# One exponential over two PSUM banks in place of two: a step of a state-space convolution kernel

## The chip, the cores and the metric

The program runs on one core of one Trainium2 chip. A core has a matrix engine (PE, with its weight loads shown apart as PEld), a vector engine (DVE), a scalar engine for activation functions (ACT), a general engine (POOL) and a queue that issues transfers (SP), each with its own instruction stream; they wait for each other by semaphores. Matrix products land in PSUM, which has eight banks of 512 float32 columns per partition. The metric is the device time of one execution in microseconds, lower is better.

## The reference

The reference is a block with adaptive layer norms around a diagonal state-space convolution (S4D) and a token-mixing MLP, in float32. This change touches the generation of the convolution kernel K, in `_A_ref`:

```python
def _A_ref(u, log_A_real, A_imag, C_real, C_imag, log_dt, D_skip):
    L = u.shape[1]                                   # L, D, N = 2048, 448, 256
    dt = jnp.exp(log_dt)
    A = -jnp.exp(log_A_real) + 1j * A_imag
    C = (C_real + 1j * C_imag) * dt[:, None]
    pos = jnp.arange(L)
    P = jnp.exp((A * dt[:, None])[:, :, None] * pos[None, None, :])
    K = 2.0 * jnp.einsum("dn,dnl->dl", C, P).real
    y = irfft(rfft(u_t, 2 * L) * rfft(K, 2 * L))[:, :, :L]
    return y + u * D_skip

h = layernorm(x) * (1 + ca) + sa
x = x + ga * _A_ref(h, ...)
h = layernorm(x) * (1 + cb) + sb
x = x + gb * mixer_mlp(h)        # W2 gelu(W1 LN(h)^T), over the tokens
```

## The kernel before, in words

The time axis is split as 32 x 64 positions, so that the exponential of a channel and state at any position is a product of a factor E (64 positions, complex) and a factor G (32 positions, complex), and K is a sum over states of E times G, a matrix product. The generator works through 56 **steps** s (28 groups of 16 channels, two halves of 128 states each). What one step does, with its lines:

- `st_exponents` (matmuls in `halves`, L627): PE computes from a short list of parameters (`lex`) and a table (`tab`) the exponents of the magnitudes, 512 columns for E (`xe`) and 512 for G (`xg`), each in a PSUM bank of its own.
- `st_exp` (L650): ACT takes the exponential of each, into `mag`, 128 x 2 x 512 in SBUF.
- `st_phase` (L627): PE computes the phases the same way into tiles of the same names, with eight matmuls of 512 columns that alternate between xe and xg; two pairs of them round the phase with a large constant (`mg`).
- `st_mag2` (L666, L671): POOL makes the magnitudes of the upper 32 positions of E, `m2`.
- `st_step`: ACT forms sines and cosines (L683 and L684 absolute values of xe and xg; L685 sine of xe, in place; L686 sine of xg into `gs`; L687 cosine for G in `gs`; L688 cosine for E, written over xg); POOL multiplies G (L690, L691); DVE multiplies E (L692, L693 with the sine, L695, L696 with the cosine). Between L693 and L695 `between()` lets DVE do work of other parts: evictions `yt` (L555) and `uo` (L589), products `z` (L817), and pieces of the parameter chains.
- `st_kgen` (L717): PE forms 64 small products of E and G in the bank `kg`; every second step ACT copies the bank out (L731).

Steps come in batches of 8. A **window** ahead of each batch computes all 8 magnitudes, since exponentials and sines need different function tables on ACT: it alternates `st_exponents` of the next step on PE with `st_exp` on ACT. In the batch, step s issues on PE the phase of step s + 1 and the kernel matmuls of step s - 2 (s - 1 after step 32), then ACT, POOL and DVE work of step s. Around this, other work is woven in by the order of the program: the transforms of the input u (L552, L585), the transforms of K (L755, copies L761), and from step 33 on the products in the frequency domain (`piece`: kx L809, z L817, vv L832, copies vt L842). The order on PE, ACT, DVE and POOL is that of the program text (`manual_schedule`); only SP's is chosen by the scheduler. After the generator (about 346 us) come the second half of the pieces and then the MLP.

PSUM is full: three banks for the transforms (`pms`), four for the tiles of the exponents and phases (`pph`, two names with two buffers each), one for kg. A tile's buffer is given to the next tile of that name when all that read or write the tile are done.

Of the kernel before, what the change touches and what calls it, by code (L numbers as in the profile page):

```python
# [11 lines left out]
F32 = mybir.dt.float32  # L12
F32R = mybir.dt.float32r
BF16 = mybir.dt.bfloat16
AF = mybir.ActivationFunctionType
# [7 lines left out]
P = 128  # L23
# [209 lines left out]
def tile_adaln_s4d_mixer(ctx, tc, i, out):  # L233
    nc = tc.nc
    x = i["A_u"][0]
# [17 lines left out]
    with ExitStack() as es:  # L253
        V, S, G, T = nc.vector, nc.scalar, nc.gpsimd, nc.tensor
# [13 lines left out]
        pph = kgen.enter_context(tc.tile_pool(name="pph", bufs=2, space=PSUM))  # L268
# [27 lines left out]
        tab = cg.tile([P, 3, 512], F32R, name="tab")  # L296
# [27 lines left out]
        lex = [cg.tile([P, N], F32R, name=f"lex{k}") for k in range(4)]  # L324
# [195 lines left out]
        nm = xp.tile([P, 16], F32, name="nm")  # L520
# [81 lines left out]
        mags, m2s, eg, phs = {}, {}, {}, {}  # L602
# [20 lines left out]
        def halves(out, lhs, rhs, start, stop):  # L623

            for k in range(2):
                r = slice(64 * k, 64 * k + 64)
                T.matmul(out[k], lhs[r], rhs[r], start=start, stop=stop)  # L627
# [12 lines left out]

        def st_exponents(s):
            g, h = divmod(s, 2)
            phs[s] = [pph.tile([P, 512], F32, tag=nm, name=nm) for nm in ("xe", "xg")]
            halves(phs[s], lex[g % 4][:, h * P : (h + 1) * P], tab[:, 2], True, True)

        def st_exp(s):
            mags[s] = mp.tile([P, 2, 512], F32, tag="mag", name="mag")
            pm = phs.pop(s)
            for k in range(2):
                S.activation(mags[s][:, k], pm[k], AF.Exp)  # L650

        def st_phase(s):

            g, h = divmod(s, 2)
            lhs = lph[g % 3][:, h * P : (h + 1) * P]
            pm = [pph.tile([P, 512], F32, tag=nm, name=nm) for nm in ("xe", "xg")]
            halves(pm, lhs, tab[:, 1], True, False)
            halves(pm, mg[:, 0], ones, False, False)
            halves(pm, mg[:, 1], ones, False, False)
            halves(pm, lhs, tab[:, 0], False, True)  # L660
            phs[s] = pm
# [347 lines left out]
        def window(s):  # L1009
# [9 lines left out]
            if s == 0:  # L1019
                st_exponents(s)  # L1020
            for e in range(BATCH):
                st_exp(s + e)

                if e + 1 < BATCH:
                    st_exponents(s + e + 1)
                else:
                    st_phase(s)
# [53 lines left out]
        for s in range(tail):  # L1081
# [30 lines left out]
            if s >= NHALF:  # L1112
                flush(dve)
                mellow()
            else:
                if s < 32 and s % BATCH > 1:
                    st_kgen(s - 2)
                if s % BATCH < 2:
                    warm(10)
                if (s + 1) % BATCH:  # L1120
                    st_phase(s + 1)
                elif s + 1 < NHALF:
                    st_exponents(s + 1)
                if s == 7:
                    warm(10)

                if s > 32 and s % BATCH:
                    st_kgen(s - 1)
                st_step(s, between)
# [122 lines left out]
    with ExitStack() as es:  # L1252
        es.enter_context(tc.manual_schedule(engines={ENG.PE, ENG.Activation, ENG.DVE, ENG.Pool}))
        V, S, G = nc.vector, nc.scalar, nc.gpsimd
# [212 lines left out]
```

## Time and profile before

| | |
|---|---|
| median of 3 runs | 696.14 us (693.27 to 698.49) |
| span of the profiled execution | 693.5 us; no other time of that execution is given |
| generator, seven batches of 8 steps | about 15 to 346 us of the span |
| exponentials L650 | 112 operations of 128x512, mean 614 ns (xe) and 617 ns (xg) |
| sines and absolute values L683 to L688 | 56 each, means of 604 to 645 ns |
| products of E on DVE, L692 to L696 | 56 each, means of 677 to 684 ns |
| PE, ACT, DVE, POOL busy | 91%, 64%, 63%, 39% of the span |

Busy times of an engine add up its operations even where they overlap; ACT operations that follow each other closely start 0.48 us apart and last 0.6. A row of the order of time gives the start (us from the span's start), the duration, the engine, the line, the operation and what it writes and reads; in square brackets stands idle time of the engine ahead of it, and what ended it. The chain of waits is the work that ended last, followed back from the end.

### The profile page before, as it was taken

To read this page: it belongs to the slowest core of one execution; us is meant where nothing else is said; L and a number is where in the kernel's file an instruction comes from. 1 tells how busy PE (TensorE), PEld (TensorE's weight loads), DVE (VectorE), ACT (ScalarE), POOL (GpSimd) and SP (SyncE) were. 2 spreads that over 40 slices of the span, in tenths; PEclk is the share of its full clock that TensorE was granted. 3 is DMA by queue.
4 is the path that set the end of the run, shared out by engine and by line. 5 is a ranking of instruction groups with operands and counts; after the bars stand their busy time and mean duration, and the time that the engine had idled before them with its cause. 6 is when DMAs were issued, how large, how long until landed. Compare 5 with 4: busy or idle time off the path is not lost.

```text
span 693.5 us, 19319 instructions
## 1 busy us (share of the span) xinstructions
PE 628.4 (91%) x7706; PEld 452.3 (65%) x7706; DVE 438.7 (63%) x835; ACT 446.6 (64%) x847; POOL 269.7 (39%) x349
## 2 busy tenths in 40 slices
PE   0878999999888889988898899999999999999997
PEld 0444555444345545555554567778899999999997
DVE  7886789789785574856745578876732364444441
ACT  5888598999689889989856768887322352222220
POOL 7694669588499667767635300000000000000000
PEclk9989999999999899999899999999999999999999
DMA  7595557598786354443479899955574445556540
GB/s 174 176 208 130 196 186 247 200 225 258 219 253 189 94 131 140 131 125 104 116 251 341 280 269 261 262 151 142 177 226 108 146 132 160 160 162 170 163 131 26
DMA packets 100322, 125.16 MB, mean 180 GB/s; under 512 B 13860, under 2 KB 81992, under 8 KB 100232
## 3 DMA queue, kind: packets, MB, share of 16 engines
q1 hardware_dynamic: 99288, 121.30, 61.0%
q0 software_dynamic: 944, 2.62, 1.6%
q8 instruction: 61, 1.00, 0.6%
q14 instruction: 29, 0.24, 0.1%
HBM read 88.53 MB, written 34.87 MB: 178 GB/s over the span
## 4 chain that ended last, share of the span: by engine, by line
PE 62%; ACT 12%; POOL 8%; DMA 6%; DVE 5%; issue 5%; SPq 1%; DVEq 0%; POOLq 0%; ACTq 0%
PE o L1434 7%; PE acc L1270 6%; PE o L1433 6%; PE o L1435 6%; PE acc L1271 6%; PE acc L1272 6%; PE xe L627 5%; PE kg L717 4%; POOL G L691 3%; POOL G L690 2%; PE xg L627 2%; PE vv L832 2%; PE kx L809 2%; PE kg L639 2%; PE y L1307 2%
## 5 line engine op out<-in xcount | busy, mean ns | idle before, releaser
L218 ACT CAST whi<-w 128x896 fp32r<-128x896 f32 x64 | 59.7, 938 | 134.3 <-PE o L1434 82.6
L227 DVE TENSOR_TENSOR wlo<-w,whi 128x896 fp32r<-128x896 f32 x64 | 68.1, 1085 | 40.6 <-ACT whi L218 40.6
L690 POOL TENSOR_TENSOR G<-mag,gs 128x512 f32<-128x512 f32 x56 | 71.8, 1282 | 46.0 <-ACT gs L686 45.9
L1270 PE MATMUL acc<-h3h,whi 128*128 128x448 f32 x224 | 82.9, 370 | 1.7 <-ACT h3h L1337 0.9
L1271 PE MATMUL acc<-h3l,whi 128*128 128x448 f32 x224 | 81.6, 364 | 0.2 <-DVE mean L1291 0.2
L1434 PE MATMUL o<-ul,whi 128*128 128x448 f32 x224 | 81.3, 363 | 0.0
L1433 PE MATMUL o<-uh,whi 128*128 128x448 f32 x224 | 81.2, 362 | 0.0
L1272 PE MATMUL acc<-h3h,wlo 128*128 128x448 f32 x224 | 80.7, 360 | 0.0
L1435 PE MATMUL o<-uh,wlo 128*128 128x448 f32 x224 | 80.6, 360 | 0.0
L717 PEld LDWEIGHTS kg<-E,G 128*32 128x32 f32 x3584 | 58.1, 117 | 31.7 <-issue 22.1
L717 PE MATMUL kg<-E,G 128*32 128x64 f32 x3584 | 68.2, 231 | 4.1 <-issue 4.1
L691 POOL TENSOR_TENSOR G<-mag,gs 128x512 f32<-128x512 f32 x56 | 71.8, 1281 | 0.0
L627 PE MATMUL xg<-tab,lph 64*128 64x512 f32 x112 | 62.9, 561 | 8.0 <-DVE E L696 3.5
L627 PE MATMUL xe<-tab,lph 64*128 64x512 f32 x112 | 63.6, 568 | 1.9 <-ACT gs L687 0.9
L1438 DVE TENSOR_TENSOR y<-o,x 128x448 f32<-128x448 f32 x16 | 10.0, 624 | 78.8 <-PE o L1435 78.8
L692 DVE TENSOR_TENSOR E<-m,xe 128x512 f32<-128x512 f32 x53 | 36.3, 684 | 35.2 <-ACT xe L685 25.1
L671 POOL TENSOR_TENSOR m<-mag,w 128x512 f32<-128x512 f32 x53 | 55.8, 1052 | 4.1
L1270 PEld LDWEIGHTS acc<-h3h,whi 128*128 128x128 f32 x224 | 42.0, 188 | 15.2 <-ACT h L1342 3.5
L817 DVE TENSOR_TENSOR z<-kx,u 128x448 f32<-128x448 f32 x48 | 28.4, 619 | 33.1 <-PE kx L809 30.5
L832 PE MATMUL vv<-z,si 64*64 64x224 f32 x512 | 36.8, 385 | 9.4 <-ACT yk L761 6.2
L627 PE MATMUL xe<-tab,lex 64*128 64x512 f32 x56 | 31.0, 569 | 15.7 <-POOL wm L874 14.8
L1433 PEld LDWEIGHTS o<-uh,whi 128*128 128x128 f32 x224 | 42.1, 188 | 3.4
(242 smaller groups left out, 1455.9 us busy)
## 6 DMA issues: line engine op xcount, KB each, us to landing
w<-in_B_w_dram SPq DMA_DIRECT2D x64, 224.0 KB
w<-in_B_w_dram SPq DMA_DIRECT2D x32, 448.0 KB
yu_d<-yt SPq DMA_DIRECT2D x16, 448.0 KB
yi<-yu_d SPq DMA_DIRECT2D x32, 224.0 KB
us_d<-uo SPq DMA_DIRECT2D x16, 448.0 KB
u<-us_d SPq DMA_DIRECT2D x64, 112.0 KB
v_d<-vt SPq DMA_DIRECT2D x32, 224.0 KB
vt<-v_d SPq DMA_DIRECT2D x14, 448.0 KB
```

The source lines that it names most:

```text
L218: self.nc.scalar.copy(hi, w)
L227: eng.tensor_tensor(lo, w, hi.bitcast(F32), ALU.subtract)
L627: T.matmul(out[k], lhs[r], rhs[r], start=start, stop=stop)
L690: G.tensor_tensor(Gt[:, 1], mg_, v32(sg), ALU.mult)
L691: G.tensor_tensor(Gt[:, 0], mg_, v32(cg_), ALU.mult)
L717: T.matmul(kg[32 * q : 32 * q + 32, m], Gt[:, c, d], E[:, c, d], start=h == 0 and c == 0 and m == 0, stop=h == 1 and c == 1, skip_group_ch ...
L1270: nc.tensor.matmul(acc[f], hi[:, fs], h3h[:, r], start=r == 0, stop=False)
L1271: nc.tensor.matmul(acc[f], hi[:, fs], h3l[:, r], start=False, stop=False)
L1272: nc.tensor.matmul(acc[f], lo[:, fs], h3h[:, r], start=False, stop=r == 15)
L1433: nc.tensor.matmul(o, hi[:, ks], uh[kh][:, k], start=kh == 0 and k == 0, stop=False)
L1434: nc.tensor.matmul(o, hi[:, ks], ul[kh][:, k], start=False, stop=False)
L1435: nc.tensor.matmul(o, lo[:, ks], uh[kh][:, k], start=False, stop=kh == 1 and k == 6)
```

## The change

The two tiles xe and xg of a step become one tile x of 128 x 2 x 512 float32, two neighbouring banks, still with two buffers, so that PSUM use is the same. The two exponentials become one operation of 1024 columns. The phases use a tile of the same name: x[:, 0] takes the place of xe and x[:, 1] that of xg; the operations on them stay as they were.

```diff
         def st_exponents(s):
             g, h = divmod(s, 2)
-            phs[s] = [pph.tile([P, 512], F32, tag=nm, name=nm) for nm in ("xe", "xg")]
-            halves(phs[s], lex[g % 4][:, h * P : (h + 1) * P], tab[:, 2], True, True)
+            phs[s] = pph.tile([P, 2, 512], F32, tag="x", name="x")
+            halves([phs[s][:, 0], phs[s][:, 1]], lex[g % 4][:, h * P : (h + 1) * P], tab[:, 2], True, True)
 
         def st_exp(s):
             mags[s] = mp.tile([P, 2, 512], F32, tag="mag", name="mag")
             pm = phs.pop(s)
-            for k in range(2):
-                S.activation(mags[s][:, k], pm[k], AF.Exp)
+            S.activation(mags[s], pm, AF.Exp)
 
         def st_phase(s):
 
             g, h = divmod(s, 2)
             lhs = lph[g % 3][:, h * P : (h + 1) * P]
-            pm = [pph.tile([P, 512], F32, tag=nm, name=nm) for nm in ("xe", "xg")]
+            x = pph.tile([P, 2, 512], F32, tag="x", name="x")
+            pm = x[:, 0], x[:, 1]
             halves(pm, lhs, tab[:, 1], True, False)
```

The order of the instructions on PE, DVE, ACT and POOL is the same, apart from the exponentials; what changes is what they wait for. The names in brackets are the semaphores that an instruction waits for: those of an engine (Activation is ACT) or of a transfer queue (DMAHW). An instruction whose data is known to be ready from an earlier wait on its engine has none.

DVE in step 44, before:

```order
L692 TENSOR_TENSOR E<-m_4662,xe 128x16x32 [waits PE_49,Activation_49,Pool_49]
L693 SCALAR_TENSOR_TENSOR E<-mag,xe 128x16x32
L817 TENSOR_TENSOR z_5096<-kx,u 128x448 [waits DMAHW4_49,DMAHW3_49,DMAHW5_49,DMAHW2_49,PE_49]
L817 TENSOR_TENSOR z_5098<-kx,u 128x448
L695 TENSOR_TENSOR E<-mag,xg 128x16x32 [waits Activation_49]
L696 TENSOR_TENSOR E<-m_4662,xg 128x16x32
```

and in the changed kernel:

```order
L692 TENSOR_TENSOR E<-m_4531,x 128x16x32 [waits PE_49,DVE_49,Activation_49,Pool_49]
L693 SCALAR_TENSOR_TENSOR E<-mag,x 128x16x32
L817 TENSOR_TENSOR z_4954<-kx,u 128x448 [waits DMAHW4_49,DMAHW3_49,DMAHW5_49,DMAHW2_49,PE_49]
L817 TENSOR_TENSOR z_4956<-kx,u 128x448
L695 TENSOR_TENSOR E<-mag,x 128x16x32
L696 TENSOR_TENSOR E<-m_4531,x 128x16x32
```

The wait for ACT ahead of L695 is gone; the one wait for ACT stands ahead of L692.

ACT in step 44 up to the copy of kg, before:

```order
L683 ACTIVATE ab<-xe 128x512 [waits PE_49,Activation_49]
L684 ACTIVATE gs<-xg 128x512 [waits PE_49,Pool_49]
L685 ACTIVATE xe<-xe 128x512 [waits DVE_49]
L686 ACTIVATE gs<-xg 128x512 [waits Pool_49]
L687 ACTIVATE gs<-gs 128x512 [waits Activation_49]
L688 ACTIVATE xg<-ab 128x512 [waits DVE_49,Activation_49]
L731 COPY ks<-kg 128x256 [waits PE_49]
```

and in the changed kernel:

```order
L683 ACTIVATE ab<-x 128x512 [waits PE_49,Activation_49]
L684 ACTIVATE gs<-x 128x512 [waits Pool_49]
L685 ACTIVATE x<-x 128x512 [waits DVE_49,Activation_49]
L686 ACTIVATE gs<-x 128x512 [waits Activation_49,Pool_49]
L687 ACTIVATE gs<-gs 128x512
L688 ACTIVATE x<-ab 128x512 [waits Activation_49]
L731 COPY ks<-kg 128x256 [waits PE_49]
```

L685 and L686 each have a wait for ACT's own semaphore that they did not have, and L684 and L687 have lost one.

PE at the start of the phase matmuls of step 46, behind the last products vv of a piece, before:

```order
L832 MATMUL vv<-z_5098,si 64x224 x3
L627 MATMUL xe<-tab,lph_144 128x512 [waits DMAHW4_49,Activation_49]
L627 MATMUL xg<-tab,lph_144 128x512 [waits DMAHW5_49,DVE_49,Activation_49]
L627 LDWEIGHTS mg
L627 MATMUL xe<-ones,mg 128x512
```

and in the changed kernel:

```order
L832 MATMUL vv<-z_4956,si 64x224 x3
L627 MATMUL x<-tab,lph_144 128x512 [waits DMAHW4_49,DVE_49,Activation_49]
L627 MATMUL x<-tab,lph_144 128x512 [waits DMAHW5_49]
L627 LDWEIGHTS mg
L627 MATMUL x<-ones,mg 128x512
```

The wait for DVE has moved from the second matmul to the first.

## The prediction

> **What bounds the kernel now.** I read the page's busy shares first, then the stages of the part that the change touches, then the chain of waits, and last the order of time of single steps.
>
> ```profile
> span 693.5 us, 19319 instructions
> PE 628.4 (91%) x7706; PEld 452.3 (65%) x7706; DVE 438.7 (63%) x835; ACT 446.6 (64%) x847; POOL 269.7 (39%) x349
> ```
>
> The change is confined to the generator of the convolution kernel, which ends near 346 us: seven batches of 8 steps, each batch opened by a window of 8 exponentials. Two stages of it (us, then busy us of PE, PEld, DVE, ACT and POOL, the granted clock, DMA share, GB/s):
>
> ```profile
> 88.00:120.00 32.00, 31.33 (x570) 18.07 (x568) 30.73 (x53) 28.34 (x55) 27.40 (x31) 1.00 0.66 218
> 271.00:300.00 29.00, 24.91 (x597) 15.75 (x595) 22.20 (x36) 28.11 (x60) 20.79 (x19) 1.00 0.48 139
> ```
>
> In the first, four engines are busy 86 to 98% of the time; in the second ACT is busy for 28.11 of 29.00 us, but operations overlap, so that busy isn't bound. The chain of waits says what binds. In the first stage it runs through POOL, without a gap:
>
> ```profile
> 104.79 1.23 POOL G L690
> 106.02 1.25 POOL G L691
> 107.27 0.20 POOL w L666
> ...
> 108.55 1.28 POOL G L690
> ```
>
> One step there is 108.55 - 104.79 = 3.76 us. In the second stage no engine is gapless, and a loop over two steps binds. These are the rows of step 43 and the start of step 45, in order of time (start, duration):
>
> ```profile
> 282.51 0.60 ACT L683 ACTIVATE ab<-xe 128x512 f32<-128x512 f32 x1
> 283.00 0.60 ACT L684 ACTIVATE gs<-xg 128x512 f32<-128x512 f32 x1
> 283.48 0.61 ACT L685 ACTIVATE xe<-xe 128x512 f32<-128x512 f32 x1
> 283.99 0.61 ACT L686 ACTIVATE gs<-xg 128x512 f32<-128x512 f32 x1
> 284.19 0.69 DVE L692 TENSOR_TENSOR E<-m,xe 128x512 f32<-128x512 f32 x1
> 284.80 0.68 DVE L693 SCALAR_TENSOR_TENSOR E<-mag,xe 128x512 f32<-128x512 f32 x1
> 284.99 0.62 ACT L688 ACTIVATE xg<-ab 128x512 f32<-128x512 f32 x1
> 285.64 0.69 DVE L695 TENSOR_TENSOR E<-mag,xg 128x512 f32<-128x512 f32 x1 [0.16 <-ACT xg L688]
> 286.24 0.68 DVE L696 TENSOR_TENSOR E<-m,xg 128x512 f32<-128x512 f32 x1
> ...
> 287.28 0.49 PE L627 MATMUL xe<-tab,lph 64*128 64x512 f32 x1
> ...
> 287.88 0.58 PE L627 MATMUL xg<-tab,lph 64*128 64x512 f32 x1
> ...
> 288.39 1.10 PE L717 MATMUL kg<-E,G 128*32 128x64 f32 x64
> ...
> 289.56 0.37 ACT L731 COPY ks<-kg 128x256 f32<-128x256 f32 x1 [0.44 <-PE kg L717]
> ...
> 289.82 0.60 ACT L683 ACTIVATE ab<-xe 128x512 f32<-128x512 f32 x1
> ```
>
> The loop: DVE's last product (L696) ends at 286.92 and frees the PSUM tiles of step 43; PE's phase matmuls of step 45 (287.28 to 288.46) and the kernel matmuls of step 43 (to 289.49) follow; ACT copies those out and only then starts step 45, 289.82 - 282.51 = **7.31 us** after step 43. What the reader should see: DVE's first two products run at 284.19 and 284.80, right after the sine of xe (L685) and beside the later ACT operations. That overlap is what the change touches.
>
> **The change, part by part.**
>
> *The order.* Both halves of a step now are one tile, x. In the changed program L695 waits for nothing any more, though it reads what L688 writes; so the wait before L692, ahead of it on DVE, already covers L688. Likewise L685 and L686 on ACT each have a wait for ACT itself that they did not have: the sine written into one half waits for the operation that read the other, and the read of the other half waits for that sine. And the first phase matmul waits for DVE as the second did. The waits follow the tile, not the half. No row of another engine moves; SP's rows change places a little, for loads that have four steps of lead, which I cost at nothing: four steps of PE, ACT and DVE work, some 15 us, hide them, and a load that came later than that would cost what PE's phase then waits.
>
> *The exponentials.* 56 pairs of 512 columns become 56 of 1024. The slope comes from an ACT operation with 896 columns, the spacing from the pairs themselves:
>
> ```profile
> L218 ACT CAST whi<-w 128x896 fp32r<-128x896 f32 x64 | 59.7, 938 | 134.3 <-PE o L1434 82.6 <-PE acc L1271 32.2 <-DMA w<-in_B_w_dram 19.5
> ```
> ```profile
> 265.85 0.62 ACT L650 ACTIVATE mag<-xg 128x512 f32<-128x512 f32 x1
> 266.33 0.63 ACT L650 ACTIVATE mag<-xe 128x512 f32<-128x512 f32 x1
> 266.81 0.64 ACT L650 ACTIVATE mag<-xg 128x512 f32<-128x512 f32 x1
> ```
>
> (938 - 610)/384 = 0.85 ns a column, so one of 1024 takes about 0.61 + 512 x 0.00085 = 1.05 us (an estimate; no row has two banks of this length). Two of today's, 0.48 apart, take 0.96 from start to start. The gain per pair lies between 1.22 - 1.05 = +0.17 (were nothing overlapped) and 0.96 - 1.05 = -0.09 (were the new one not overlapped with the next); nearest to the spaced rows, with the same overlap of 0.14, it is 0.05. Of the windows most wait for PE; where ACT paces them (about 20 of the 56) this is **-1 us**; bounds -9.5 and +5.
>
> The Trainium skill's page "ScalarE: Activation LUTs", section "What ACT_TABLE_LOAD costs", puts such an operation at 186 ns + 0.833 ns a column, with back-to-back ones overlapping by about 93 ns. By that this term would be at most 56 x 93 ns = -5.2 us. Its slope agrees with 0.85; its spacing (520 ns) is above the 480 here, and the row decides.
>
> *The waits on ACT.* What an ACT operation pays for waiting on the one just ahead is shown by two pairs of 256 columns, the first dependent, the second not:
>
> ```profile
> 11.45 0.42 ACT L917 ACTIVATE xa<-ya 128x256 f32<-128x256 f32 x1
> 11.89 0.42 ACT L918 ACTIVATE xa<-xa 128x256 f32<-128x256 f32 x1
> ```
> ```profile
> 87.10 0.42 ACT L407 ACTIVATE xa<-A_C_real 128x256 f32<-128x256 f32 x1
> 87.42 0.40 ACT L407 ACTIVATE ya<-A_C_imag 128x256 f32<-128x256 f32 x1
> ```
>
> 0.44 against 0.32: +0.12, twice a step: L683 to the end of L688 grows from 3.10 to **3.34 us**.
>
> *The wait on DVE.* In the loop above L692 then starts 0.06 after L688's end, and the four products, 0.60 apart, end 3 x 0.60 + 0.68 = 2.48 us later. From L696's end to the next L683 it stays 289.82 - 286.92 = 2.90. Sum: 3.34 + 0.06 + 2.48 + 2.90 = **8.78 us** instead of 7.31, +1.47 for two steps. Of it 0.36 could hide in PE's kx matmuls, which now end before the wait; I leave it, as z, the product between L693 and L695 in even steps, comes later by as much. A batch has three such loops, with 0.13 in its first step and 0.24 in its last ACT chain: 3 x 1.47 + 0.4 = 4.8. The batches from 227, 271 and 314 us: 3.8 in the first, where PE is late already (clock and weights) in one loop, 4.8, and 4.8 + 1.2 in the last, whose last E comes that much later beyond its ACT chain: **+14.6**.
>
> In the stage that POOL binds, step 13 to step 15 reads:
>
> ```profile
> 108.13 0.60 ACT L683 ACTIVATE ab<-xe 128x512 f32<-128x512 f32 x1 [0.47 <-PE xe L627]
> ...
> 110.88 0.59 ACT L688 ACTIVATE xg<-ab 128x512 f32<-128x512 f32 x1
> ...
> 111.31 1.87 DVE L555 SCALAR_TENSOR_TENSOR yt<-pu,mod 128x448 f32<-128x448 f32 x3
> ...
> 113.69 0.68 DVE L696 TENSOR_TENSOR E<-m,xg 128x512 f32<-128x512 f32 x1
> 114.61 0.49 PE L627 MATMUL xe<-tab,lph 64*128 64x512 f32 x1
> ...
> 115.89 0.60 ACT L683 ACTIVATE ab<-xe 128x512 f32<-128x512 f32 x1
> ```
>
> 7.76 us. Here three evictions of 0.60 stand between the products; L692 does not overlap them any more with ACT. After: 3.34 + 0.06 + 2.48 + 1.80 + 1.52 (114.37 to 115.89) = 9.2, and with the 0.24 that PE need not wait, 9.0: more than POOL's two steps of 3.76. With two evictions (even steps, and all steps of the next two batches) 8.4. So POOL's cover ends after the first loop of a batch, whose L683 has 0.5 to 0.7 of slack, and the loops cost +1.2 each. The batches at 88, 138 and 183 us: 3.2 (less what POOL held back L688 at its end), 4.0 (its end waits for DVE's uo, behind L692) and 3.5 (waits of PE for its own instructions hide some): **+10.7**. The batch at 28 us has the slow clock and such waits in it: **+1.7**, the least certain term.
>
> **Sum:** -1 + 14.6 + 10.7 + 1.7 = 26; I take 2 off for waits of PE that nothing shows, which a later loop may hide: +24. On the profiled span 693.5 + 24 = 717.5; the median of the runs, 696.14, stands 2.6 above the span (what lies around the span, and the scatter of 693.27 to 698.49), so 696.1 + 24 = **720 us**.
>
> **The rivals.**
>
> *POOL still covers the first four batches.* For it: the gapless chain of 3.76 us steps, and 10.7 us of my sum stand against it. Against: 8.4 to 9.0 is more than 7.5. If ACT's results reach POOL no later than now there, -1 + 14.6 + 1.7 less 2 = +13: 709. Chance 0.18.
>
> *The clock falls more often.* PE would idle more, and after idling its phase matmuls are slow:
>
> ```profile
> 52.67 0.43 PE L717 MATMUL kg<-E,G 128*32 128x64 f32 x6 [2.53 <-issue]
> 53.03 0.79 PE L627 MATMUL xe<-tab,lph 64*128 64x512 f32 x1
> ...
> 54.15 0.98 PE L627 MATMUL xe<-tab,lph 64*128 64x512 f32 x1
> ```
>
> 53.03 to 55.13 is 2.10, against 1.18 at 287.28. The new waits of PE are at most some 1.4 us long, half the 2.53 here; but with one slow loop a batch (phase +0.9, kernel matmuls about as much again) it is 7 x 1.6 = 11 more: 731. Chance 0.12.
>
> *The waits follow the bank, and the change is not slower.* If L692 could start 0.1 after L685 as now (it decides whether L692 starts before L688's end), all loops stay and the exponentials alone count: 696.1 minus 1, to 9.5 at the bound: 687 to 695, on the other side. For it: the halves are separate banks, and nothing in the data asks for more. Against: L695's missing wait. The Trainium skill's page "PSUM — Partial Sum Buffer", section "PSUM bank collisions raise a hardware error", asks for a guard by bank and quadrant only, by which this would be the time; the program's rows speak for a guard by tile. Chance 0.06.
>
> **How the numbers follow.** The forecast, 715 to 727, has 0.60; POOL's cover (704 to 714) 0.18; the clock (728 to 737) 0.12; the bank rival 0.06; 0.04 remain for a cover in between that leaves it near 700. The range must reach both neighbours: 706 to 733, which leaves out the bank rival and the outer parts of the others. A measurement of this kernel tells some 1% (7 us) from no change. Faster by over 1%, under 689: half the bank rival, 0.03. Within 1%: the other half and the 0.04: 0.07. Slower: 0.90.
>
> **What would show it.** L649 as 56 operations near 1.05 us. L692 starting some 0.06 after L688's end in every step, and the idle time before it, now 35.2 us and mostly put down to L685, grown and put down to L688:
>
> ```profile
> L692 DVE TENSOR_TENSOR E<-m,xe 128x512 f32<-128x512 f32 x53 | 36.3, 684 | 35.2 <-ACT xe L685 25.1 <-issue 3.6 <-POOL G L691 2.9
> ```
>
> L685 and L686 come 0.61 after their predecessors. L683 to L683 over two steps 8.4 to 9.0 us. The end of the generator near 371 us instead of 346; nothing changed behind it. I am wrong if L692 keeps starting right after L685, if POOL stays gapless between 88 and 120 us, or if the half clock spreads.

## The result: 743.73 us, 6.8% slower, and the profile after

| | before | changed |
|---|---|---|
| median (4 runs each) | 694.70 us (690.38 to 698.49) | 743.73 us (736.94 to 747.50) |
| ratio | | 1.068, 95% interval 1.063 to 1.073 |
| span of the profiled execution | 693.5 us | 745.7 us |

The forecast of 720 us had the direction and the wait that causes the loss, but only half the size; 743.73 lies above the range that ended at 733. First the busy shares of the changed kernel, then the same two stages as before the change (the batches of steps 8 to 15 and 40 to 47; columns us, busy us of PE, PEld, DVE, ACT and POOL, clock, DMA share, GB/s):

```profile
span 745.7 us, 19243 instructions
PE 632.7 (85%) x7706; PEld 454.4 (61%) x7706; DVE 435.7 (58%) x835; ACT 454.9 (61%) x791; POOL 269.1 (36%) x349
...
92.60:127.00 34.40, 29.16 (x496) 17.11 (x495) 25.08 (x44) 26.05 (x48) 25.19 (x28) 0.90 0.46 150
308.00:338.00 30.00, 22.14 (x464) 13.90 (x462) 17.15 (x29) 25.51 (x51) 18.25 (x19) 0.94 0.40 116
```

The matmuls, products and sines are the same, and every engine idles more: DVE and POOL, busy 30.73 and 27.40 of 32.00 us in the first stage before, now have 25.08 and 25.19 of 34.40. The groups of instructions say what they wait for (busy us, mean ns | idle time before them):

```profile
L690 POOL TENSOR_TENSOR G<-mag,gs 128x512 f32<-128x512 f32 x56 | 71.5, 1276 | 81.0 <-ACT gs L686 81.0
L692 DVE TENSOR_TENSOR E<-m,x 128x512 f32<-128x512 f32 x53 | 36.4, 687 | 87.4 <-issue 44.8
L649 ACT ACTIVATE mag<-x 128x1024 f32<-128x1024 f32 x56 | 55.5, 1024 | 26.4 <-PE x L627 24.9
```

The wait before L692 grew from 35.2 to 87.4 us. Half of it is put down to "issue", but in 43 of the 56 steps L692 starts 0.09 to 0.11 us after L688's end, whichever of the two the row names (in the others 0.03 to 0.50). So it is in the late loop of two steps, steps 43 to 45 again:

```profile
322.66 0.61 ACT L683 ACTIVATE ab<-x 128x512 f32<-128x512 f32 x1
323.15 0.60 ACT L684 ACTIVATE gs<-x 128x512 f32<-128x512 f32 x1
323.78 0.58 ACT L685 ACTIVATE x<-x 128x512 f32<-128x512 f32 x1
324.46 0.60 ACT L686 ACTIVATE gs<-x 128x512 f32<-128x512 f32 x1
...
325.47 0.59 ACT L688 ACTIVATE x<-ab 128x512 f32<-128x512 f32 x1
...
326.15 0.69 DVE L692 TENSOR_TENSOR E<-m,x 128x512 f32<-128x512 f32 x1 [2.12 <-issue]
...
327.95 0.68 DVE L696 TENSOR_TENSOR E<-m,x 128x512 f32<-128x512 f32 x1
...
328.78 0.50 PE L627 MATMUL x<-tab,lph 64*128 64x512 f32 x2 [1.53 <-DVE E L696]
...
331.06 0.37 ACT L731 COPY ks<-kg 128x256 f32<-128x256 f32 x1 [1.18 <-PE kg L717]
...
331.32 0.60 ACT L683 ACTIVATE ab<-x 128x512 f32<-128x512 f32 x1
```

331.32 - 322.66 = 8.66 us instead of 7.31. The products no longer run beside ACT's operations but behind them.

What had not been counted stands in the first stage. DVE, then PE, then ACT, steps 12 to 14:

```profile
116.28 0.69 DVE L692 TENSOR_TENSOR E<-m,x 128x512 f32<-128x512 f32 x1 [2.99 <-issue]
116.89 0.68 DVE L693 SCALAR_TENSOR_TENSOR E<-mag,x 128x512 f32<-128x512 f32 x1
117.49 1.28 DVE L555 SCALAR_TENSOR_TENSOR yt<-pu,mod 128x448 f32<-128x448 f32 x2
118.68 0.68 DVE L695 TENSOR_TENSOR E<-mag,x 128x512 f32<-128x512 f32 x1
119.28 0.68 DVE L696 TENSOR_TENSOR E<-m,x 128x512 f32<-128x512 f32 x1
```
```profile
118.22 2.46 PE L552 MATMUL pu<-xt,wur 64*128 64x449 f32 x4 [1.88 <-DVE yt L555]
120.61 1.65 PE L717 MATMUL kg<-E,G 128*32 128x64 f32 x64
122.19 0.51 PE L627 MATMUL x<-tab,lph 64*128 64x512 f32 x2
```
```profile
123.47 0.60 ACT L683 ACTIVATE ab<-x 128x512 f32<-128x512 f32 x1 [0.77 <-PE x L627]
```

The evictions yt stand behind L692 on DVE. PE's transform of u (pu) waits for the bank that they free, and ahead of the phases in PE's order stand that transform and kgen: the phases of step 14 could have started when L696 ended, at 119.96, and start at 122.19. Behind the wait of 1.88 us the clock was at half as well (0.53 from 118.20 to 121.60), so that the four pu took 2.46 us and the kernel matmuls 1.65. From L683 of step 12 (112.80) to that of step 14 it is 10.67 us, where 9.0 was forecast.

The starts of L683 divide the generator (us; a window runs from the last L683 of a batch to the first of the next):

| run | steps 0 to 7 | 8 to 31, three batches | 32 to 55, three batches | six windows |
|---|---|---|---|---|
| before | 30.3 | 81.7 | 79.4 | 120.0 |
| changed | 30.8 | 99.9 | 96.7 | 134.1 |
| e1, two exponentials | 31.7 | 101.2 | 96.4 | 133.5 |
| e2, bank pairs alternate | 30.8 | 97.7 | 95.6 | 128.2 |
| e3, two tiles, cosine products first | 31.0 | 96.7 | 92.5 | 126.5 |
| e4, e2 + evictions first | 30.0 | 83.9 | 98.9 | 128.2 |
| e10, e4 + cosine fifth | 30.1 | 83.2 | 90.3 | 123.9 |
| e15, e10 + two exponentials | 29.7 | 83.9 | 90.6 | 122.7 |
| e16, e15 with two tiles | 28.6 | 82.3 | 84.0 | 122.3 |

With 0.6 us before the first step and 1.6 us behind the last L683, the differences between the first two rows add up to the 52.2 us of the spans, within rounding.

### The profile page after: what moved, and what is told of

Read it like the earlier page. It is cut to its first block, busy times and chain, and to the rows that moved or that the text cites. A ratio compares the mean times of both kernels' runs of the same rounds, so it can differ in the third digit from the quotient of the medians.

```text
span 745.7 us, 19243 instructions
## 1 busy us (share of the span) xinstructions
PE 632.7 (85%) x7706; PEld 454.4 (61%) x7706; DVE 435.7 (58%) x835; ACT 454.9 (61%) x791; POOL 269.1 (36%) x349
## 5 line engine op out<-in xcount | busy, mean ns | idle before, releaser
L690 POOL TENSOR_TENSOR G<-mag,gs 128x512 f32<-128x512 f32 x56 | 71.5, 1276 | 81.0 <-ACT gs L686 81.0
L627 PE MATMUL x<-tab,lph 64*128 64x512 f32 x224 | 66.5, 574 | 32.6 <-ACT gs L686 10.5
L692 DVE TENSOR_TENSOR E<-m,x 128x512 f32<-128x512 f32 x53 | 36.4, 687 | 87.4 <-issue 44.8
L717 PEld LDWEIGHTS kg<-E,G 128*32 128x32 f32 x3584 | 63.5, 125 | 33.4 <-issue 19.2
L717 PE MATMUL kg<-E,G 128*32 128x64 f32 x3584 | 73.4, 244 | 3.0 <-issue 3.0
L691 POOL TENSOR_TENSOR G<-mag,gs 128x512 f32<-128x512 f32 x56 | 71.7, 1280 | 0.0
L649 ACT ACTIVATE mag<-x 128x1024 f32<-128x1024 f32 x56 | 55.5, 1024 | 26.4 <-PE x L627 24.9
L627 PE MATMUL x<-tab,lex 64*128 64x512 f32 x112 | 35.0, 606 | 31.6 <-DMA lex<-wm 18.1
L627 PEld LDWEIGHTS x<-tab,lph 64*128 64x128 f32 x224 | 24.4, 199 | 53.1 <-ACT x L685 16.4
L683 ACT ACTIVATE ab<-x 128x512 f32<-128x512 f32 x56 | 33.6, 600 | 21.0 <-PE x L627 20.5
```

The source lines that it names most:

```text
L690: G.tensor_tensor(Gt[:, 1], mg_, v32(sg), ALU.mult)
L691: G.tensor_tensor(Gt[:, 0], mg_, v32(cg_), ALU.mult)
L717: T.matmul(kg[32 * q : 32 * q + 32, m], Gt[:, c, d], E[:, c, d], start=h == 0 and c == 0 and m == 0, stop=h == 1 and c == 1, skip_group_ch ...
```

## The experiments

Theory A: the loss is the new wait of L692 for the last operation on the joint tile, and what queues behind L692. Theory B: a good part of it is the one exponential and the late release of its banks. Theory C: the lower clock. Ratios are to the kernel before, with 95% intervals; medians of 4 runs unless said.

**e1: two exponentials on the joint tile.**

```diff
-            S.activation(mags[s], pm, AF.Exp)
+            for k in range(2):
+                S.activation(mags[s][:, k], pm[:, k], AF.Exp)
```

> The changed kernel, but with the two exponentials of 512 columns as before; the joint tile of two banks stays. Theory A (the loss is the wait of the first product L692 for the last sine L688, and what queues behind it on VectorE): the exponentials have no part in it, 742 to 747 us. Theory B (a good part of the loss, the 14.7 us by which the windows between batches grew, comes from the one exponential, which gives back both banks only at its end): about 729 us.

748.34 us, ratio 1.080 (1.076 to 1.085): not less than the changed kernel. The windows are as long (133.5 against 134.1 us). Theory B falls. By the ratios e1 is even 1.2% slower than the changed kernel; why stays open, and e15 and e10 below, the same comparison on another base, do not show it.

**e2: the joint tile alternates between its two bank pairs.** In the changed program the allocation of buffers does not alternate at two places: x of step 25 got the banks of step 24, and x of step 33 those of step 32.

```diff
-            ... pph.tile([P, 2, 512], F32, tag="x", name="x")
+            ... pph.tile([P, 2, 512], F32, tag=f"x{s % 2}", name="x", bufs=1)
```

> The changed kernel with the joint tile of step s always in bank pair s mod 2. In the changed kernel steps 24 and 25, and 32 and 33, were given the same pair, and at 191.6 us TensorE waited 2.4 us for the exponential of step 24 there. If those two repeats are what made the windows ahead of steps 24 and 32 longer (4.5 and 1.5 us), the time is 738 to 741 us; if the next waits take their place, 743 to 744 us.

736.92 us, ratio 1.063 (1.059 to 1.067). The row of PE's order of time that prompted it, in the changed kernel, and the place in e2:

```profile
191.59 0.80 PE L627 MATMUL x<-tab,lex 64*128 64x512 f32 x2 [2.41 <-ACT mag L649]
```
```profile
189.35 1.86 PE L755 MATMUL y<-wc,ks 64*64 64x64 f32 x62 [2.32 <-DVE uo L589]
191.23 0.79 PE L627 MATMUL x<-tab,lex 64*128 64x512 f32 x2
```

The wait for the exponential is gone, but at this place PE now waits as long for an eviction (uo), which stands behind L692 on DVE. The window ahead of step 24 fell from 24.20 to 20.83 us, that ahead of step 32 did not fall (16.06, 17.24). By the profiles the windows are 5.9 us shorter; by the ratios it is 3.5 us in all, within the error of the two (4.5). So it is small. 736.92 lies below both forecasts: the batch of steps 24 to 31, too, went from 35.4 to 30.8 us. Four of its steps, 26 to 30, in the changed kernel and in e2 (columns as above, the clock third from the end):

```profile
218.40:238.80 20.40, 17.24 (x334) 8.71 (x333) 14.31 (x25) 13.87 (x27) 14.94 (x16) 0.83 0.46 146
```
```profile
214.80:232.10 17.30, 15.12 (x332) 7.39 (x336) 14.43 (x25) 13.86 (x27) 14.86 (x17) 1.00 0.71 230
```

The program's order is the same, and L692 waits for L688 in both, but in e2 the clock is full. One of these loops in the changed kernel, then in e2:

```profile
223.84 1.45 PE L585 MATMUL pu<-yi,s 64*64 64x448 f32 x6 [1.58 <-DVE uo L589]
225.22 1.93 PE L717 MATMUL kg<-E,G 128*32 128x64 f32 x64
```
```profile
220.24 0.98 PE L585 MATMUL pu<-yi,s 64*64 64x448 f32 x6 [1.12 <-DVE uo L589]
221.14 1.10 PE L717 MATMUL kg<-E,G 128*32 128x64 f32 x64
```

So the loop is 8.65 us at full clock and 10.19 with a stretch of half clock in it.

**e3: the wait alone, in the kernel before.** Two tiles, two exponentials; DVE's order changes, so that its first product needs L688. (The tiles also alternate by step, as in e2; e13 shows that this changes nothing. The same holds for e8, e12 and e16.)

```diff
-            V.tensor_tensor(E[:, 1, :, 32:64], m2, se, ALU.mult)
-            V.scalar_tensor_tensor(E[:, 1, :, 31::-1], ..., se, ALU.mult, ALU.mult)
-            between()
             V.tensor_tensor(E[:, 0, :, 31::-1], me[:, :, 31::-1], ce, ALU.mult)
             V.tensor_tensor(E[:, 0, :, 32:64], m2, ce, ALU.mult)
+            between()
+            V.tensor_tensor(E[:, 1, :, 32:64], m2, se, ALU.mult)
+            V.scalar_tensor_tensor(E[:, 1, :, 31::-1], ..., se, ALU.mult, ALU.mult)
```

> The kernel before, two tiles and two exponentials, with the four products of a step in another order on VectorE: the two cosine products first, then the evictions, then the two sine products. Its first product so waits for L688, as in the changed kernel, while ScalarE has none of the waits from L684 to L685 and from L685 to L686. The tiles alternate by step. Theory A: most of the loss comes back, 725 to 740 us (the changed kernel less the 0.3 us a step of ScalarE). Theory B, or a loss by ScalarE's own waits: 695 to 705 us.

731.68 us, ratio 1.057 (1.053 to 1.061). Its first product (now with the cosine, at L692) shows the mark of the changed kernel:

```profile
L692 DVE TENSOR_TENSOR E<-mag,xg 128x512 f32<-128x512 f32 x56 | 38.5, 687 | 77.7 <-ACT xg L688 77.5
```

Neither a joint tile nor a fused exponential is needed: with the wait of DVE's first product come some 39 us. This is the run that decides for A. Two things come with the wait and are not separated from it here: xe, which L693 freed before, is now the last to be freed, and the half-clock time is 61.4 us instead of 30.7 (71.7 in the changed kernel).

**e4: e2 with the evictions ahead of L692** (`between()` moved up two lines).

> The changed kernel with alternating bank pairs and with the evictions (yt, uo, z) ahead of L692 on VectorE, not behind L693: they no longer stand behind the wait for L688. Theory A with the queue as its main part (evictions come late, TensorE's in-order matmuls of pu, kx and vv wait for their banks, and the phases of the next step stand behind those): the batches from 8 and 24 lose their period of 10 to 11 us for two steps, 715 to 725 us. If only the wait of the products themselves counts: within 3 us of the run with alternating bank pairs.

724.27 us, ratio 1.047 (1.043 to 1.050), by the ratios 11.5 us less than e2. PE's order of time in the batch of steps 8 to 15:

```profile
105.14 1.15 PE L552 MATMUL pu<-xt,wur 64*128 64x449 f32 x4
106.22 1.10 PE L717 MATMUL kg<-E,G 128*32 128x64 f32 x64
```

The transform that took 2.46 us behind a wait of 1.88 takes 1.15, at full clock, and waits for nothing. Steps 8 to 31 return to 83.9 us (81.7 before), and their half-clock time to 3.4 us (17.0 in e2, 20.4 in the changed kernel, 3.4 before); the late batches, where two products z stand there in every other step, gain nothing (98.9). So the queue behind L692, with the clock that falls with it, is most of the loss of the early batches, and the wait itself that of the late ones.

**e8: the same edit in the kernel before, as a control** (10 runs).

> A control: the kernel before (alternating tiles) with the evictions ahead of L692. Its L692 waits little, so by theory A there is nothing to gain: 690 to 700 us. If the evictions come too late for reasons of their own, and the 12.6 us that the same edit brought in the changed kernel have nothing to do with its wait, it gains as much here: about 680 us.

692.73 us, ratio 0.996 (0.993 to 0.999): 3 us, not 11.5. The evictions' place matters because of the wait in front of them. It is the fastest of all, by less than the 1% that this kernel's measurement tells.

**e10 and e11: when the last operation on the joint tile ends.** On top of e4, ScalarE's order changes. e10: L686, L685, L688, L687, so that the operations on x end at 2.9 us after L683; e11: L686, L687, L685, L688, one dependent pair less.

```diff
             S.activation(cg_, xg, AF.Abs)
-            S.activation(xe, xe, AF.Sin, scale=TWO_PI)
             S.activation(sg, xg, AF.Sin, scale=-TWO_PI)
-            S.activation(cg_, cg_, AF.Sin, scale=-TWO_PI, bias=math.pi / 2)
+            S.activation(xe, xe, AF.Sin, scale=TWO_PI)
             S.activation(xg, ab, AF.Sin, scale=-TWO_PI, bias=math.pi / 2)
+            S.activation(cg_, cg_, AF.Sin, scale=-TWO_PI, bias=math.pi / 2)
```

> The run with alternating pairs and evictions first, with ScalarE's last four operations of a step in the order L686, L685, L688, L687: the last operation on the joint tile ends at about 2.9 us after L683, not 3.4, while ScalarE's step stays at about 3.4 us (two dependent pairs in a row, as now), and GpSimd has its first sine 0.5 us earlier. Theory A (what is left, 29 us by the profile, most of it in the batches from step 32 on, is VectorE's wait for the last operation on the joint tile): 0.5 us of a loop of two steps in the late batches, 12 loops, and some in the windows: 712 to 720 us. If ScalarE's own time or its own waits are what is left: 723 to 727 us.

> The same base with the order L686, L687, L685, L688: one dependent pair in a row and not two, so that ScalarE's step is 3.25 us and not 3.4; the last operation on the joint tile is again the last of the step, at 3.25 us. Theory A: 0.15 us for VectorE's wait, a third of what the run with the cosine fifth brings, 720 to 723 us. If ScalarE's own waits are what is left: more than that run, 712 to 718 us.

e10: 712.48 us, ratio 1.026 (1.020 to 1.031); e11: 717.76 us, ratio 1.032 (1.025 to 1.039). In e10 and e4 the idle time before the first product of DVE (at L693 there) is:

```profile
L693 DVE TENSOR_TENSOR E<-m,x 128x512 f32<-128x512 f32 x53 | 36.3, 685 | 45.7 <-POOL G L690 25.7
```
```profile
L693 DVE TENSOR_TENSOR E<-m,x 128x512 f32<-128x512 f32 x53 | 36.3, 686 | 62.0 <-ACT x L688 29.8
```

Half a microsecond per step in the wait is worth 12 us of median, most of it in the late batches (98.9 to 90.3): A. e11 gained 6.5 us, more than the 1 to 4 that A expects of 0.15 us. ScalarE's own waits may weigh as well, or GpSimd's earlier start: with L686 first, its first sine is done 0.8 us earlier in e10 and in e11. In the kernel before that gained nothing (e12), but there VectorE's sine came later; these parts are not separated.

**e14: e10's order of ScalarE alone, in the changed kernel.**

> The changed kernel with nothing but the order of ScalarE's last four operations changed (L686, L685, L688, L687). Theory A: the wait of L692 and all that stands behind it, the evictions too, end 0.5 us earlier in each step: 12 us as with evictions first, and more where the evictions hold TensorE, 715 to 730 us. If the evictions' place behind L692 is what counts, whatever the wait: 733 to 740 us.

722.65 us, ratio 1.040 (1.032 to 1.047): as A has it. The half-clock time of steps 8 to 31 falls to 3.4 us here too, although the evictions still stand behind L692.

**e15, e16, e13: what remains.** e15 is e10 with two exponentials, e16 is e15 with two tiles, e13 the kernel before with alternating tags (10 runs).

> The best run with the joint tile (alternating pairs, evictions first, cosine fifth), but with two exponentials of 512 columns. Against that run it shows what the one exponential is worth: by the prediction 1 us, within bounds of -9.5 and +5, so 711 to 716 us; if it is worth the 8 us that the ratios of the first runs suggest, about 721 us.

> The same as the run before this one, but with two tiles: L692 waits for the sine of xe alone, 0.5 us later than in the kernel before, L695 for the cosine, 0.5 us earlier. Theory A: what remains of the loss is the joint tile's, 688 to 698 us. If the new order on ScalarE holds the remaining loss: 705 to 715 us.

> A control: the kernel before, with its two tiles in banks that alternate by step, as in the runs that build on alternating tiles. Nothing else is changed; 692 to 698 us by every theory.

e15: 712.09 us, ratio 1.028 (1.022 to 1.033), against 712.48 of e10. One exponential or two makes no difference that can be told, as the forecast's -1 had it. e13: 695.39 us, ratio 1.001 (0.997 to 1.005): the tags change nothing. e16 ran at 688.57, 699.14, 699.85 and 700.45 us, too far apart for a ratio; the median, 699.49, is just above the 688 to 698 of theory A. All four lie below e15's lowest, 711.17, by 10.7 us or more: so much the joint tile alone still costs there. It was not tried to give the halves separate waits within one tile.

**e5, e6, e7: the cosine out of the joint tile.** L688 writes into E's own cosine part in SBUF, and the product is made there in place; E is two tiles. e5 in the changed kernel, e6 in the kernel before, e7 is e5 with evictions first.

```diff
-            S.activation(xg, ab, AF.Sin, scale=-TWO_PI, bias=math.pi / 2)
-            se, ce = v32(xe), v32(xg)
+            ce = E[0][:, :, 32:64]
+            S.activation(ce, v32(ab), AF.Sin, scale=-TWO_PI, bias=math.pi / 2)
+            se = v32(xe)
...
-            V.tensor_tensor(E[:, 0, :, 32:64], m2, ce, ALU.mult)
+            V.tensor_tensor(ce, m2, ce, ALU.mult)
```

> The changed kernel (joint tile, one exponential), but the cosine of L688 goes to SBUF, into the half of E's cosine part that the product with m2 fills afterwards (E is two tiles, E0 and E1, so that this is no dependency of the sine products). L692 then waits for L686, the last reading of the joint tile on ScalarE (2.4 us after L683 and not 3.4), and the tile is free after L693. Theory A (what the joint tile costs is the wait of VectorE for L688 and the late release after L696, no more): the loss is gone, and the release is earlier than in the kernel before, 680 to 700 us. Theory B (ScalarE's own waits, the clock and the shared banks hold the loss): 715 to 735 us.

> The kernel before (two tiles, two exponentials) with the cosine of L688 in E's cosine part in SBUF. L692 waits for L685 as before; xg is free after L686 and not after L696 of its step. Theory A, where the release of xg after L696 holds the phases of the step after next: 675 to 692 us. If ScalarE and GpSimd set these steps already: 690 to 695 us.

> The run with the joint tile and the cosine in E, with the evictions ahead of L692 as well. If the evictions still stand behind a waiting L692 there: 3 to 10 us less than that run. If nothing waits behind L692 any more: within 3 us of it, or longer, since the sine products and with them the release of the tile come behind the evictions.

e5 719.76 us (ratio 1.036, 1.030 to 1.041), e6 718.25 (1.031, 1.027 to 1.036), e7 717.79 (1.034, 1.028 to 1.039). Alone, e5 would speak for B. But e6, with two tiles and every wait of the kernel before, is as slow: the remedy has a price of its own. Groups of e6, then of the kernel before (lines are shifted by one: L697 is the product with m2, L692 the second of GpSimd):

```profile
L692 POOL TENSOR_TENSOR G<-mag,gs 128x512 f32<-128x512 f32 x56 | 85.6, 1528 | 0.0
L697 DVE TENSOR_TENSOR E<-m,E 128x512 f32<-128x512 f32 x53 | 68.2, 1286 | 1.8
L666 POOL TENSOR_TENSOR w<-mag 128x16 f32<-128x16 f32 x56 | 21.1, 376 | 9.7 <-ACT mag L650 7.9 <-DVE z L818 1.5
```
```profile
L691 POOL TENSOR_TENSOR G<-mag,gs 128x512 f32<-128x512 f32 x56 | 71.8, 1281 | 0.0
L696 DVE TENSOR_TENSOR E<-m,xg 128x512 f32<-128x512 f32 x53 | 35.9, 678 | 0.0
L666 POOL TENSOR_TENSOR w<-mag 128x16 f32<-128x16 f32 x56 | 13.8, 247 | 11.6 <-ACT mag L650 11.4
```

The same product takes 1286 ns with both inputs in SBUF and 678 with one in PSUM, and GpSimd's take 1528 instead of 1281. Between e5 and e6, where that price is the same, joint tile and one exponential cost 0.4%, within the error, instead of 6.8%: with the cosine out of the tile that loss is gone, as A says, or hidden behind the new price, by which the 680 to 700 us expected of e5 were missed. e7 gains nothing on e5 that can be told, since no long wait stands at L692 any more.

**e9: more matmuls, for the clock**, on top of e2.

```diff
+            if h == 0:
+                warm(7)
             if h == 1:
                 p, o = divmod(g, 2)
```

> The run with alternating bank pairs, with seven more matmuls of ones into the unused half of kg after the first kgen of each pair, as they already stand in the windows, to keep TensorE at work. It is about the clock: TensorE's records show half the clock for 58 us between the first L683 and the last in that run, 31 us in the kernel before. Theory C (a good part of the loss is the lower clock that the new waits bring): the half-clock time falls below 35 us and the run is 8 to 15 us under that with alternating pairs alone. Theory A (the waits are the loss, the clock follows them): within 4 us of it, or longer by up to 28 times the 0.9 us that seven such matmuls take, where TensorE was not idle there.

753.08 us, ratio 1.084 (1.077 to 1.090). Time at half clock between the first and the last L683 fell only from 58 to 51 us, and the matmuls cost more than was idle. It does not test theory C.

**e12: e8 with L686 ahead of L685** (10 runs).

> The kernel before with alternating tiles and evictions first (0.996 of the kernel before), with L686 ahead of L685 on ScalarE: GpSimd has its sine 0.5 us earlier and VectorE its own 0.5 us later. If GpSimd's two products set the batches from 8 to 31: 683 to 690 us. If VectorE's sine products set them: 694 to 702 us.

696.16 us, ratio 1.003 (0.999 to 1.007): GpSimd's earlier start does not pay for VectorE's later one. No version beats the kernel before by more than can be told; e8 is the nearest.

## Why the prediction came to half of the loss

| term | predicted | profile |
|---|---|---|
| exponentials and windows | -1 | +14.1, and 0.6 before the first step |
| batches 32 to 55 | +14.6 | +17.3 |
| batches 8 to 31 | +10.7 | +18.2 |
| first batch | +1.7 | +0.4 |
| waits of PE that may be hidden | -2 | none seen |
| outside the generator | 0 | +1.6 |

- **The order and the waits: right.** L692 behind L688 by 0.09 (0.06 predicted); L683 to the end of L688 3.40 us (3.34), and in the late loop L684 to L685 0.63 and L685 to L686 0.68 (0.61). e3 and e16 confirm that this wait is the cause.
- **Late loops: right in mechanism, near in size.** 8.66 us for 8.78. Beyond the forecast the three batches lost 2.7 us. Their half-clock time is 13.6 us instead of 3.5, three more stretches of 3.4 us; the loop from step 49, with one, takes 9.81 us and that from step 51, with none, 8.66. That is enough for the 2.7.
- **Early batches: the step that failed is "9.0 with three evictions, 8.4 with two".** It let the phases start when L696 ends, and took PE as free and at full clock then. It had DVE's queue behind L692 only as a delay of L696, not of the banks that the evictions free. The loop is 10.67 in steps 12 to 14, and in steps 26 to 30, with two evictions, 10.2. In steps 12 to 14 the phases start 2.23 us after L696's end. PE came to the transform at 118.22; from there to the phases it took 3.97 us, where the same work takes 2.18 in e4 (105.14 to 107.32) at full clock. So some 1.8 us of the 2.23 are the clock and 0.4 the late start, an estimate from these rows. Where the clock was full the forecast was near: 8.62 to 8.66 us in steps 19 to 23, 8.65 in steps 26 to 30 of e2, for 8.4. e4 takes the queue away, and wait and half clock go together: +2.2 instead of +18.2 us.
- **First batch: near by luck.** +0.4 us for +1.7, but before the change this batch had 10.2 us of half clock, and in the profile of the changed kernel none.
- **Windows: the step that failed is that they contain exponentials alone.** The price of one exponential was right (1024 ns for an estimate of 1050; e15). But a window's first matmuls wait for the last products of the batch before, and PE works in order. In the window after step 7, on PE and ACT:

```profile
63.66 0.71 PE L627 MATMUL x<-tab,lex 64*128 64x512 f32 x2 [2.74 <-ACT x L688]
64.30 2.31 PE L639 MATMUL kg<-ones 128*128 128x256 bf16 x10
```
```profile
66.65 0.37 ACT L731 COPY ks<-kg 128x256 f32<-128x256 f32 x1 [2.91 <-PE kg L639]
```

  The exponents of step 8 need the tile of step 6, whose L696 ended at 63.56; the matmuls into kg stand behind them, ACT's copy of kg behind those, and the table loads and all exponentials behind the copy. Before, this copy was at 62.63 (L683 of step 7 then at 58.81, now 59.88), so 3.0 us are lost in this one chain. Some 1.0 of them is the clock: the ten matmuls into kg take 2.31 us here and 1.26 before. In all windows the half-clock time is 37.5 us instead of 13.5. What a stretch costs there shows the window ahead of step 48, 18.48 us with two of them and 15.65 in e2 with none: 1.4 us each. e2 takes the windows from 134.1 to 128.2 us, with 23.9 us of half clock, e10 to 123.9.
- **The clock: the term that the sum left out.** "With one slow loop a batch" stood for 11 us and had a chance of 0.12, as a case beside the forecast, on the ground that the new waits of PE are at most some 1.4 us long. In the loops of steps 10 to 14 they were 1.90 and 1.88 us, in those of steps 26 to 30 1.58 and 1.57, and the three loops of steps 24 to 30 all had a stretch of half clock. Half-clock time between the first and last L683 is 71.7 us, 30.7 before: twelve more stretches of 3.4 us. At 1.1 to 1.5 us each (the pairs above: late loops, windows, steps 26 to 30) they are 13 to 18 of the 52.2 us, an estimate. Another one agrees: within the runs of each of the 18 kernels the span falls by some 4.7 us for each 0.01 of granted clock (correlation -0.81); the medians are 0.949 for the changed kernel and 0.978 before, by that slope about 13 us. No run changed the clock alone, so how much of it the waits bring about stays open; in e4 and e14, where the wait or the queue is shorter, it is less in the early batches.
- **POOL's cover** did end, as forecast: its idle time at L690 went from 45.9 to 81.0 us. **Waits by bank** did not occur.

## What to carry to other kernels

Joining two tiles joins their waits: before fusing two operations, list for each consumer which is the last producer on the joint tile, and compare that wait with the few tens of nanoseconds that the fusion can save. Follow an added wait through the queue behind it to the buffers that this queue frees, and through the in-order engine that waits for them, in the stretches between the loops too. Where waits grow, count a lower clock as a term of the sum, not as another case, and read the granted clock of a slow loop before its whole excess is put down to the wait.

## What the runs showed of the hardware

- **Half clock without long idle.** In the batch of steps 8 to 15 no single wait of PE is longer than 1.90 us, yet the clock halves in stretches of 3.4 us (columns as above):

```profile
104.50:107.90 3.40, 1.50 (x8) 0.51 (x4) 2.46 (x5) 3.25 (x7) 3.32 (x5) 1.00 0.08 26
107.90:111.30 3.40, 3.40 (x68) 2.03 (x66) 3.40 (x7) 0.87 (x2) 3.31 (x4) 0.54 0.74 216
111.40:118.20 6.80, 4.94 (x94) 2.70 (x86) 3.81 (x8) 5.50 (x11) 4.38 (x7) 0.99 0.49 153
118.20:121.60 3.40, 3.38 (x44) 1.86 (x48) 3.40 (x6) 1.42 (x3) 3.40 (x4) 0.53 0.38 150
```

  The stretch ahead of the first one has PE busy for 1.50 of 3.40 us. In e2's steps 26 to 30, with waits of 1.06 and 1.12 us, the clock stayed at 1.00. What share of busy time decides was not measured. The Trainium skill's page "TensorE: Matmul & The Clock Gate", section "HAM oscillation — how this bites in real kernels", gives as the rule that idle gaps above some 3.4 us are to be avoided; here the clock halved with no gap above 1.90 us.
- **Two SBUF inputs on VectorE beside GpSimd.** The product with m2 goes from 678 to 1286 ns, the other cosine product from 677 to 962, and GpSimd's from 1281 to 1528 (e6). The Trainium skill's page "SBUF — State Buffer", section "SBUF: two separate sides", says that a VectorE operation with two SBUF inputs and a GpSimd operation that reads SBUF lock each other out for a whole instruction; the trace agrees, in that both got slower at once.
